# A linear-attention plus maxout-FFN kernel on one core: PSUM banks dealt by earliest predicted release, E and F loaded over the ACT queue, parts of the attention work moved

## The chip, the core and the metric

The kernel runs on one NeuronCore of a Trainium2 chip. The metric is device time in microseconds (us). The names are those of the profile: PE is TensorE's matrix multiply, PEld its weight load, DVE is VectorE, ACT is ScalarE, POOL is GpSimd, and SP is the engine that only issues DMAs here. The *granted clock* is the share of TensorE's full clock that the profile's records show. A run is "fast" unless its time is over 1.5% above the fastest run of the same kernel; only fast runs are compared.

## The reference

```python
# q, k, v: (8 batches, 8 heads, 1024, 64); E, F: (64, 1024)
k_proj = einsum('ks,bhsd->bhkd', E, k);  v_proj = einsum('ks,bhsd->bhkd', F, v)
attn   = softmax(q @ k_proj.T / sqrt(64))          # 64 keys only
x      = (attn @ v_proj), heads side by side       # (8192 tokens, 512)
h      = max(x @ w1, x @ w2, x @ w3)               # (8192, 768)
out    = h @ w_out                                 # (8192, 512)
```

The FFN is nearly all of the work: per batch 144 matmuls of 128x512 for w1 to w3 and 48 for w_out.

## The kernel before

Every engine's instruction order is written out by hand. A batch has two chunks of 512 tokens. A chunk has six *up* steps (12 matmuls each, into three PSUM banks) and four *down* steps (6 matmuls each, into one bank). Attention of the *next* batch is slipped in behind these steps by a plan: `(chunk, step): [work]`. The work items are `kproj`/`vproj` (multiply by E and F), `kt` and `qp` (transposes on PE), `qd` (four DVE copies into `q_p`, then a DMA transpose into `qT`), `sc` (scores, then exp on ACT), and `za` (sums and values on PE, reciprocal on ACT as ln and exp, multiply on DVE).

PE writes into eight PSUM banks. (The Trainium skill, "PSUM — Partial Sum Buffer", section "Specifications (TRN2)", gives 8 banks of 512 FP32 values per partition, and the kernel's tile has that shape.) A bank can be written again only when ACT or DVE has read it. The kernel deals the banks while it is built, with a small model of when each engine will be done (shortened here; `...` and the comments are mine):

```python
psum_t = psum.tile([P, 8, 512], FP32, name="banks")
clock = {"pe": 0.0, "s": 0.0, "v": 0.0}     # predicted time of PE, ACT, DVE
free = [0.0] * 8                            # predicted release of each bank

def two():                                  # an even-odd pair, for sums, values, scores, transposes
    n = min(range(0, 8, 2), key=lambda n: max(free[n:n + 2]))
    deal((n, n + 1)); return psum_t[:, n:n + 2, :], (n, n + 1)

def bank():                                 # one bank, for up, down, kproj, vproj
    def rank(n):
        ready = free[n] <= clock["pe"]
        return (not ready, ready and free[n ^ 1] <= clock["pe"], free[n])
    n = min(range(8), key=rank)
    deal((n,)); return psum_t[:, n, :], (n,)
...
def up(b, ch, jt):
    ...                                     # banks h[0], h[1], h[2], 4 matmuls each
    nc.scalar.copy(out=h1s, in_=h[0][0])    # ACT releases h[0]
    run_later()                             # ACT: exp of the scores dealt before
    nc.vector.tensor_tensor(out=m12, in0=h[1][0], in1=h1s, op=ALU.max)   # DVE releases h[1]
    most(hTs[b, ch][:, jt, :], *h[2], m12)                               # DVE releases h[2]
```

`rank` prefers a bank that is ready by the model and whose neighbour is *not* ready, so that whole pairs stay free for `two()`.

The program starts with the loads of E, F, q, k and v, dummy matmuls (`idle(n)`, each 128x512, into a bank that nobody reads) that are meant to keep PE's clock up, and attention for the first half chunk.

The softmax here doesn't subtract the row's maximum and nothing guards it: scores larger than these inputs give would overflow.

Of the kernel before, what the change touches and what calls it, by code (L numbers as in the profile page):

```python
# [15 lines left out]
def kernel(  # L16
# [13 lines left out]
    nc = tc.nc  # L30

    B, H, S, D = q.shape
    KP = E.shape[0]
# [4 lines left out]
    P = 128  # L38
# [25 lines left out]
    clock = {"pe": 0.0, "s": 0.0, "v": 0.0}  # L64
    free = [0.0] * 8
# [11 lines left out]
        return psum_t[:, n:n + 2, :], (n, n + 1)  # L77

    def bank():
        def rank(n):  # L80
            ready = free[n] <= clock["pe"]
            return (not ready, ready and free[n ^ 1] <= clock["pe"], free[n])

        n = min(range(8), key=rank)
        deal((n,))
        return psum_t[:, n, :], (n,)

# [14 lines left out]
    def copy(eng, o, i, ns=(), dt=0.65):  # L102
        {  # L103
            "v": nc.vector.tensor_copy, "s": nc.scalar.copy, "g": nc.gpsimd.tensor_copy
        }[eng](out=o, in_=i)
        runs(eng, clock["pe"] if ns else 0.0, dt, ns)
# [40 lines left out]
    q_c = [first.tile([P, 2, SPC, 2, D], BF16, name=f"q_c{i}") for i in range(2)]  # L147
    v_heads = [(0, 4), (4, 6), (6, 8)]
    v_f = [first.tile([P, b - a, SI, D], FP32, name=f"v_f{a}") for a, b in v_heads]
    for i in range(2):  # L150
        cols = slice(i * S // 2, (i + 1) * S // 2)
        nc.sync.dma_start(out=ef_f[0:KP, cols], in_=E[:, cols])
        nc.scalar.dma_start(out=ef_f[KP:P, cols], in_=F[:, cols])
    for i in range(2):
        nc.sync.dma_start(out=q_f[i], in_=view(q, 0)[:, 4 * i:4 * i + 4, 0:SPC])
    for i in range(2):
# [43 lines left out]
    def exps(b, g, lo, nsi, sc):  # L200
        t, ns, ready = sc
        pTs[b, g, lo] = att.tile([P, 2, CHUNK], BF16, name="pT", bufs=4)[:, :, 0:nsi * HALF]
        nc.scalar.activation(out=pTs[b, g, lo], in_=t, func=AF.Exp, scale=scale)  # L203
        runs("s", ready, 0.17 + nsi * 0.107, ns)
# [14 lines left out]
    def sums(b, g, lo, nsi):  # L219
        return pair_mm(b, g, lo, nsi, lambda rows, hp: ones[rows])  # L220

    def invert(b, g, lo, nsi, z):
        t, ns, ready = z
        zl = att.tile([P, 2, CHUNK], FP32, name="zl", bufs=1)[:, :, 0:nsi * HALF]
        nc.scalar.activation(out=zl, in_=t, func=AF.Ln)  # L225
        runs("s", ready, 0.17 + nsi * 0.107, ns)
        if nsi == SI:
            zi = att.tile([P, 2, CHUNK], FP32, name="zi", bufs=2)
        else:
            zi = att.tile([P, 2, CHUNK // 2], FP32, name="zi0", bufs=4)  # L230
        nc.scalar.activation(out=zi, in_=zl, func=AF.Exp, scale=-1.0)  # L231
        zis[b, g, lo] = zi, runs("s", ready, 0.17 + nsi * 0.107)

    def values(b, g, lo, nsi):
        if b not in xTs:
            xTs[b] = att.tile([P, NCT, SI, P], BF16, name="xT")
        return pair_mm(b, g, lo, nsi, lambda rows, hp: vps[b][rows, 2 * g + hp, :])

    def scale_x(b, g, lo, nsi, av):
        t, ns, ready = av  # L240
        zi, when = zis.pop((b, g, lo))
        nc.vector.tensor_tensor(  # L242
            out=xTs[b][:, g, lo:lo + nsi, :].rearrange("a (c s) p -> a c (s p)", c=2),
            in0=t, in1=zi, op=ALU.mult,
        )
        runs("v", max(ready, when), 0.17 + nsi * 0.13, ns)
# [8 lines left out]
    def sc(b, g, lo=0, nsi=SI):  # L255
        def f():
            t = scores(b, g, lo, nsi)
            later.append(lambda: exps(b, g, lo, nsi, t))
        return f
# [66 lines left out]
    def kproj(b):  # L326
        def f():
            t, ns = bank()
            proj(b, 1, t, (LO, HI), 4 * D)
            kps[b] = att.tile([P, 2, 2 * D], BF16, name="kp")  # L330
            copy("v", kps[b].rearrange("a g x -> a (g x)"), t[:, 0:4 * D], ns, 0.43)
        return f
# [31 lines left out]
    def idle(n):  # L364

        t, ns = bank()
        for _ in range(n):
            nc.tensor.matmul(out=t, lhsT=warm[:, 0:P], rhs=warm, start=True, stop=True)  # L368
        free[ns[0]] = pe(n * MM)
# [56 lines left out]
    def v_part(i):  # L426
        a, b = v_heads[i]
        t, ns = bank()
        proj(0, 2, t, (slice(a, b), slice(a, b)), (b - a) * D)
        copy("v", vps[0][:, a:b].rearrange("a h d -> a (h d)"), t[:, 0:(b - a) * D], ns, 0.4)  # L430

    C0 = (0, SPC)
    idle(8)
    cast_q(0, "v")
    cast_q(1, "s")
    turn_ef()
    turn_q(0)
    turn_q(1)
    idle(2)
    cast_q(2, "v")  # L440
    cast_q(3, "s")
    turn_q(2)
    turn_q(3)
    idle(8)
    cast_k(0, 0, "v")
    cast_k(0, 1, "s")
    kp = k_half(0)
# [3 lines left out]
    sc01 = [scores(0, g, *C0) for g in (0, 1)]  # L451
    for g in (0, 1):
        exps(0, g, *C0, sc01[g])
    idle(4)
    cast_k(1, 0, "v")
    cast_k(1, 1, "g")
    load_w(0, 0)
    load_w(0, 1)
    for g in (0, 1):
        invert(0, g, *C0, sums(0, g, *C0))  # L460
        idle(1)
    kp = k_half(1)
    idle(2)
    k_turn(1, kp)
    idle(2)
    sc23 = [scores(0, g, *C0) for g in (2, 3)]
    for g in (2, 3):
        exps(0, g, *C0, sc23[g - 2])
    copy("v", v_t[:, 0:2], v_f[0][:, 0:2])
    copy("g", v_t[:, 2:4], v_f[0][:, 2:4])  # L470
    load_w(1, 0)
# [2 lines left out]
    nc.gpsimd.dma_start(out=q_t[:, :, SPC:], in_=view(q, 0)[:, :, SPC:])  # L474
    load_w(2, 1)
    nc.gpsimd.dma_start(out=wout_sb, in_=moe_w_out.rearrange("(jt p) m -> p jt m", p=P))
    copy("v", v_t[:, 4:6], v_f[1])
    idle(1)
    v_part(0)
    idle(1)  # L480
    for g in (2, 3):
        invert(0, g, *C0, sums(0, g, *C0))
    idle(1)
    scale_x(0, 0, *C0, values(0, 0, *C0))
    copy("v", v_t[:, 6:8], v_f[2])
    v_part(1)
    scale_x(0, 1, *C0, values(0, 1, *C0))
# [104 lines left out]
    def ld(b):  # L592
        return lambda: load(b)

    def plan(b):
        n = b + 1
        if b == 0:
            c1 = (SPC, SPC)
            return {
                (0, 5): [za(0, 0, *c1), sc(0, 2, *c1)],  # L600
                (0, 6): [za(0, 1, *c1), sc(0, 3, *c1)],
                (0, 7): [za(0, 2, *c1)],
                (0, 8): [za(0, 3, *c1), ld(1)],
                (1, 0): [kproj(1)],
                (1, 1): [kt(1), qp(1, (0,)), qp(1, (1,))],
                (1, 2): [qp(1, (2,)), qp(1, (3,)), sc(1, 0), vproj(1), ld(2)],
                (1, 3): [za(1, 0), sc(1, 1)],
                (1, 4): [za(1, 1), sc(1, 2)],
                (1, 5): [za(1, 2), sc(1, 3)],
                (1, 7): [za(1, 3)],  # L610
            }
        if b == 1:
            return {
                (0, 1): [qd(2)],
                (0, 5): [kproj(2), vproj(2), ld(3)],
                (0, 6): [kt(2)],
                (0, 7): [sc(2, 0)],
                (0, 9): [za(2, 0), sc(2, 1)],
                (1, 1): [za(2, 1), sc(2, 2)],
                (1, 3): [za(2, 2), sc(2, 3)],  # L620
                (1, 5): [za(2, 3)],
            }
        if b == 2:
            return {
                (0, 0): [qd(3)],
                (0, 2): [kproj(3), vproj(3), ld(4)],
                (0, 3): [kt(3)],
                (0, 4): [sc(3, 0)],
                (0, 6): [za(3, 0), sc(3, 1)],
                (1, 0): [za(3, 1), sc(3, 2), qd(4)],  # L630
                (1, 2): [za(3, 2), sc(3, 3), kproj(4), vproj(4), ld(5)],
                (1, 4): [kt(4)],
                (1, 5): [za(3, 3), sc(4, 0)],
            }
        if n == B:
            return {}
        out = {
            (0, 1): [za(n, 0), sc(n, 1)],
            (0, 3): [za(n, 1), sc(n, 2)],
            (0, 9): [za(n, 2), sc(n, 3)],  # L640
            (1, 3): [za(n, 3)],
        }
        if n + 1 < B:
            out[0, 2] = [qd(n + 1)]
            out[0, 9] += [kproj(n + 1), vproj(n + 1)]
            out[1, 1] = [kt(n + 1)]
            out[1, 3] += [sc(n + 1, 0)]
        if n + 2 < B:
            out[1, 1] += [ld(n + 2)]
        return out  # L650

    for b in range(B):
        p = plan(b)

        def behind(ch, step):
            for f in p.get((ch, step), []):
                f()

        for ch in range(NCHUNK):
            if (b, ch) == (0, 0):  # L660
                c1 = (SPC, SPC)
                scale_x(0, 3, *C0, values(0, 3, *C0))
                up_first({
                    (2, 1): [qp(0, (0, 1), *c1), qp(0, (2, 3), *c1)],
                    (2, 2): [sc(0, 0, *c1)],
                    (2, 3): [sc(0, 1, *c1)],
                })
                run_later()
                behind(0, NJT - 1)
            else:  # L670
                for step in range(NJT):
                    up(b, ch, step)
                    behind(ch, step)
            for tt in range(SPC):
                down(b, ch, tt, "v" if (b, ch) == (0, 0) else "s")
                behind(ch, NJT + tt)
# [30 lines left out]
```

## Time and profile before

| | |
|---|---|
| time | 418.76 us, median of 3 runs (418.64 to 419.24); 418.51 to 420.86 in later rounds |
| span of the profiled run | 416.7 us |
| PE busy | 397.6 us, 95% |
| first FFN matmul | 23.53 us |

The head of the profile's page, and its line of the chain of work that ended last (shares of the span by engine):

```profile
span 416.7 us, 6032 instructions
## 1 busy us (share of the span) xinstructions
PE 397.6 (95%) x2400; PEld 180.8 (43%) x2445; DVE 203.9 (49%) x315; ACT 193.5 (46%) x280; POOL 27.9 (7%) x37
...
PE 87%; ACT 5%; DVE 3%; DMA 2%; issue 2%; SPq 1%; DVEq 0%; ACTq 0%
```

PE is the bottleneck, so the question is what PE waits for. The waits view of PE (who waited for whom: us in total, times, longest):

```profile
PE banks L499 <- ACT zl L225: 2.1, 3, 0.7
PE banks L212 <- ACT pT L203: 1.7, 4, 0.5
PE banks L499 <- DVE vp L103: 1.5, 2, 0.8
PE banks L375 <- DMA ef_f<-in_F_dram: 1.2, 1, 1.2
...
PE banks L499 <- issue: 0.8, 5, 0.2
PE banks L284 <- DVE qT L103: 0.8, 1, 0.8
...
PE banks L192 <- ACT pT L203: 0.5, 1, 0.5
```

Here L499 is `up`, L212 sums and values, L192 scores, L375 the transposes of E and F, L284 the q transposes. A wait of `up` for "ACT zl" is a wait for a *bank*: zl is made by reading the sums' bank.

The timeline before (start, length, engine, line, operation, out<-in; in brackets the idle time before it and what ended it). The start of the program:

```profile
6.00 1.13 PE L375 MATMUL banks<-ident_f,ef_f 128*128 128x128 f32 x8 [1.20 <-DMA ef_f<-in_F_dram]
...
11.06 0.69 DVE L103 CAST k_t<-k_f_92 128x1024 bf16<-128x1024 f32 x1 [0.88 <-DMA k_f_92<-in_k_dram]
...
23.53 13.17 PE L499 MATMUL banks<-xT,w_sb 128*128 128x512 bf16 x59
```

Then the last batch, b = 7, where there is no attention at all:

```profile
375.90 0.69 DVE L509 TENSOR_TENSOR hT<-banks,m_3390 128x512 bf16<-128x512 f32 x1
376.65 2.47 PEld L499 LDWEIGHTS <-w_sb 128*128 128x128 bf16 x12 [0.20 <-issue]
...
378.57 0.69 DVE L509 TENSOR_TENSOR hT<-banks,m_3407 128x512 bf16<-128x512 f32 x1
379.32 2.47 PEld L499 LDWEIGHTS <-w_sb 128*128 128x128 bf16 x12 [0.20 <-issue]
```

The weight loads start anew at 376.65 and 379.32. That is 0.06 us after the DVE instruction that releases the previous step's last bank has ended (375.90 + 0.69 = 376.59, and 378.57 + 0.69 = 379.26). A step takes 379.32 - 376.65 = 2.67 us, and its twelve matmuls alone need 12 x 0.216 = 2.59 (24 back-to-back ones take 5.18 us in the chain of waits). The idle label says only "issue", and no waits line is longer than 0.2 us.

### The profile page before, as it was taken

What the parts mean: (1) busy time and instruction counts of PE and PEld (TensorE: products, weight loads), DVE (VectorE), ACT (ScalarE), POOL (GpSimd) and SP (SyncE); (2) the same over time, 40 slices, a digit from 0 to 9 for tenths busy, and PEclk for the clock granted to TensorE, in tenths of its full rate; (3) what the DMA queues carried; (4) which work ended last, traced back from release to release, by engine and by line L of the source; (5) the groups of instructions that cost most, each with busy time, mean ns of one, the idle gap of its engine ahead of it and who ended that gap; (6) DMA issues with size and microseconds to landing.
All of it is one profiled execution on the core that took longest, in us unless ns stands there. A gap on an engine that the chain in (4) does not pass through costs nothing.

```text
span 416.7 us, 6032 instructions
## 1 busy us (share of the span) xinstructions
PE 397.6 (95%) x2400; PEld 180.8 (43%) x2445; DVE 203.9 (49%) x315; ACT 193.5 (46%) x280; POOL 27.9 (7%) x37
## 2 busy tenths in 40 slices
PE   6999998999999999999999999999999999999996
PEld 3444453344444444444544435443454444444442
DVE  3357664464373636637263464527365272525251
ACT  2530617822764266457535546436445456432322
POOL 0621001002000200200200001000000000000000
PEclk9999999999999999999999999999999999999999
DMA  7999949958922699599793159921410202020202
GB/s 259 353 205 196 178 124 164 202 135 122 242 46 101 126 197 248 95 227 219 116 241 86 66 109 224 172 103 31 122 50 2 101 0 102 0 102 0 101 2 101
DMA packets 58492, 54.92 MB, mean 132 GB/s; under 512 B 25952, under 2 KB 51808, under 8 KB 58464
## 3 DMA queue, kind: packets, MB, share of 16 engines
q0 software_dynamic: 25296, 25.69, 39.3%
q1 hardware_dynamic: 33008, 28.58, 20.6%
q8 instruction: 19, 0.31, 0.3%
q10 hardware_dynamic: 160, 0.26, 0.2%
q14 instruction: 9, 0.07, 0.1%
HBM read 57.15 MB, written 16.78 MB: 177 GB/s over the span
## 4 chain that ended last, share of the span: by engine, by line
PE 87%; ACT 5%; DVE 3%; DMA 2%; issue 2%; SPq 1%; DVEq 0%; ACTq 0%
PE banks L499 58%; PE banks L574 19%; PE banks L212 4%; PE banks L273 4%; ACT zl L225 2%; DMA k_f_92<-in_k_dram 2%; PE banks L192 1%; ACT pT L203 1%; PE banks L368 1%; PE banks L284 1%; ACT zi L231 1%; DVE vp L103 1%; ACT o_sb L103 0%; ACT h1s L557 0%; DVE q_p L103 0%
## 5 line engine op out<-in xcount | busy, mean ns | idle before, releaser
L499 PE MATMUL banks<-xT,w_sb 128*128 128x512 bf16 x1119 | 255.1, 379 | 6.1 <-ACT zl L225 2.1
L499 PEld LDWEIGHTS <-w_sb 128*128 128x128 bf16 x1152 | 110.0, 98 | 143.2 <-issue 15.5
L557 ACT COPY h1s<-banks 128x512 f32<-128x512 f32 x90 | 52.5, 584 | 95.1 <-PE banks L499 90.7
L574 PE MATMUL banks<-wout_sb,hT 128*128 128x512 bf16 x375 | 86.1, 379 | 1.0 <-DVE vp L103 0.2
L242 DVE TENSOR_TENSOR xT<-banks,zi 128x1024 bf16<-128x1024 f32 x28 | 34.3, 1225 | 74.4 <-ACT zi L231 52.5
L103 ACT COPY o_sb<-banks 128x512 f32<-128x512 f32 x60 | 35.1, 585 | 54.8 <-PE banks L574 54.8
L574 PEld LDWEIGHTS <-hT 128*128 128x128 bf16 x384 | 36.5, 98 | 47.2 <-issue 4.6
L225 ACT ACTIVATE zl<-banks 128x1024 f32<-128x1024 f32 (+1 forms) x36 | 33.5, 930 | 31.3 <-PE banks L212 30.3
L203 ACT ACTIVATE pT<-banks 128x1024 bf16<-128x1024 f32 (+1 forms) x36 | 33.3, 931 | 14.6 <-PE banks L192 14.6
L231 ACT ACTIVATE zi<-zl 128x1024 f32<-128x1024 f32 x28 | 29.6, 1057 | 0.9
L178 POOL DMA_DIRECT2D q_t<-in_q_dram x7 | 6.2, 879 | 199.3 <-DMA qT<-q_p 64.1
L273 PEld LDWEIGHTS <-efT 128*64 128x64 bf16 x304 | 14.6, 110 | 5.2 <-issue 4.7
L212 PE MATMUL banks<-pT,ones 64*64 64x512 bf16 (+1 forms) x144 | 13.7, 374 | 1.9 <-ACT pT L203 1.7
L192 PE MATMUL banks<-qT,kpT 64*64 64x512 bf16 (+1 forms) x144 | 13.0, 359 | 0.7 <-ACT pT L203 0.5
L212 PE MATMUL banks<-pT,vp 64*64 64x512 bf16 (+1 forms) x144 | 13.3, 356 | 0.2 <-DVE vp L103 0.2
L368 PE MATMUL banks<-warm 128*128 128x512 bf16 x34 | 11.1, 440 | 1.5 <-DVE warm L162 1.2
L212 PEld LDWEIGHTS <-ones 64*64 64x64 bf16 x144 | 4.4, 103 | 15.5 <-issue 13.8
L273 PE MATMUL banks<-v_t,efT 128*64 128x256 bf16 (+1 forms) x160 | 9.6, 263 | 0.4 <-DVE v_t L103 0.3
L103 ACT CAST vp<-banks 64x256 bf16<-64x256 f32 x14 | 5.1, 365 | 10.4 <-PE banks L273 10.2
L273 PE MATMUL banks<-k_t,efT 128*64 128x256 bf16 (+1 forms) x144 | 8.9, 264 | 0.6 <-DVE k_t L103 0.5
L103 DVE CAST vp<-banks 64x256 bf16<-64x256 f32 (+2 forms) x17 | 7.0, 410 | 4.4 <-ACT vp L103 3.7
L103 DVE COPY q_p<-q_t 128x1024 bf16<-128x1024 bf16 x24 | 8.5, 419 | 0.0
(252 smaller groups left out, 219.1 us busy)
## 6 DMA issues: line engine op xcount, KB each, us to landing
out_dram<-o_sb SPq DMA_DIRECT2D x30, 512.0 KB, 3.3
k_t<-in_k_dram POOLq DMA_DIRECT2D x7, 1024.0 KB, 14.0
q_t<-in_q_dram POOLq DMA_DIRECT2D x7, 1024.0 KB, 9.8
v_t<-in_v_dram POOLq DMA_DIRECT2D x7, 1024.0 KB, 17.8
w_sb<-in_moe_w_dram POOLq DMA_DIRECT2D x6, 384.0 KB, 7.9
k_f_92<-in_k_dram SPq DMA_DIRECT2D x1, 1024.0 KB, 7.9
k_f_93<-in_k_dram SPq DMA_DIRECT2D x1, 1024.0 KB, 10.0
v_f_96<-in_v_dram SPq DMA_DIRECT2D x1, 1024.0 KB, 11.5
```

The costliest lines, as they stand in the source:

```text
L103: {"v": nc.vector.tensor_copy, "s": nc.scalar.copy, "g": nc.gpsimd.tensor_copy}[eng](out=o, in_=i)
L192: nc.tensor.matmul(out=t[c * HALF:(c + 1) * HALF, hp, 0:n * P], lhsT=kpTs[b][rows, g, :], rhs=qTs[b][rows, at:at + n, :], start=True, stop ...
L203: nc.scalar.activation(out=pTs[b, g, lo], in_=t, func=AF.Exp, scale=scale)
L212: nc.tensor.matmul(out=t[hp * HALF:(hp + 1) * HALF, c, 0:nsi * HALF], lhsT=w(rows, hp), rhs=p[rows, hp, :], start=True, stop=True,)
L225: nc.scalar.activation(out=zl, in_=t, func=AF.Ln)
L231: nc.scalar.activation(out=zi, in_=zl, func=AF.Exp, scale=-1.0)
L242: nc.vector.tensor_tensor(out=xTs[b][:, g, lo:lo + nsi, :].rearrange("a (c s) p -> a c (s p)", c=2), in0=t, in1=zi, op=ALU.mult,)
L273: nc.tensor.matmul(out=t[hh * HALF:(hh + 1) * HALF, 0:width], lhsT=efT[:, si, kv - 1, :], rhs=qkv[b][kv][:, heads[hh], si, :], start=(si = ...
L368: nc.tensor.matmul(out=t, lhsT=warm[:, 0:P], rhs=warm, start=True, stop=True)
L499: nc.tensor.matmul(out=h, lhsT=w_sb[i][:, ct, jt * P:(jt + 1) * P], rhs=xTs[b][:, ct, ch * SPC:(ch + 1) * SPC, :], start=(ct == 0), stop=( ...
L557: nc.scalar.copy(out=h1s, in_=h[0][0])
L574: nc.tensor.matmul(out=o_ps, lhsT=hTs[b, ch][:, jt, tt * P:(tt + 1) * P], rhs=wout_sb[:, jt, :], start=(jt == 0), stop=(jt == NJT - 1),)
```

## The change

Its intent: take the bank that has been free longest; take the two E issues off SP, so that q and k are issued sooner; and start attention of b = 1 one step earlier, with scores two steps ahead of their sums. It also moves `qd` (the q copies on DVE) in b = 3 to 5 from step 2 to step 4. In the prologue, `k_half(1)` goes ahead of the sums, and the dummies are shared out anew. The diff, whole:

```diff
--- before.py
+++ after.py
@@ -77,11 +77,7 @@
         return psum_t[:, n:n + 2, :], (n, n + 1)
 
     def bank():
-        def rank(n):
-            ready = free[n] <= clock["pe"]
-            return (not ready, ready and free[n ^ 1] <= clock["pe"], free[n])
-
-        n = min(range(8), key=rank)
+        n = min(range(8), key=lambda n: free[n])
         deal((n,))
         return psum_t[:, n, :], (n,)
 
@@ -147,10 +143,8 @@
     q_c = [first.tile([P, 2, SPC, 2, D], BF16, name=f"q_c{i}") for i in range(2)]
     v_heads = [(0, 4), (4, 6), (6, 8)]
     v_f = [first.tile([P, b - a, SI, D], FP32, name=f"v_f{a}") for a, b in v_heads]
-    for i in range(2):
-        cols = slice(i * S // 2, (i + 1) * S // 2)
-        nc.sync.dma_start(out=ef_f[0:KP, cols], in_=E[:, cols])
-        nc.scalar.dma_start(out=ef_f[KP:P, cols], in_=F[:, cols])
+    nc.scalar.dma_start(out=ef_f[0:KP], in_=E)
+    nc.scalar.dma_start(out=ef_f[KP:P], in_=F)
     for i in range(2):
         nc.sync.dma_start(out=q_f[i], in_=view(q, 0)[:, 4 * i:4 * i + 4, 0:SPC])
     for i in range(2):
@@ -430,18 +424,18 @@
         copy("v", vps[0][:, a:b].rearrange("a h d -> a (h d)"), t[:, 0:(b - a) * D], ns, 0.4)
 
     C0 = (0, SPC)
-    idle(8)
+    idle(9)
     cast_q(0, "v")
     cast_q(1, "s")
     turn_ef()
     turn_q(0)
     turn_q(1)
-    idle(2)
+    idle(3)
     cast_q(2, "v")
     cast_q(3, "s")
     turn_q(2)
     turn_q(3)
-    idle(8)
+    idle(7)
     cast_k(0, 0, "v")
     cast_k(0, 1, "s")
     kp = k_half(0)
@@ -451,21 +445,20 @@
     sc01 = [scores(0, g, *C0) for g in (0, 1)]
     for g in (0, 1):
         exps(0, g, *C0, sc01[g])
-    idle(4)
+    idle(2)
     cast_k(1, 0, "v")
     cast_k(1, 1, "g")
     load_w(0, 0)
     load_w(0, 1)
-    for g in (0, 1):
-        invert(0, g, *C0, sums(0, g, *C0))
-        idle(1)
     kp = k_half(1)
-    idle(2)
+    z01 = [sums(0, g, *C0) for g in (0, 1)]
+    invert(0, 0, *C0, z01[0])
     k_turn(1, kp)
     idle(2)
     sc23 = [scores(0, g, *C0) for g in (2, 3)]
-    for g in (2, 3):
-        exps(0, g, *C0, sc23[g - 2])
+    exps(0, 2, *C0, sc23[0])
+    invert(0, 1, *C0, z01[1])
+    exps(0, 3, *C0, sc23[1])
     copy("v", v_t[:, 0:2], v_f[0][:, 0:2])
     copy("g", v_t[:, 2:4], v_f[0][:, 2:4])
     load_w(1, 0)
@@ -474,14 +467,13 @@
     nc.gpsimd.dma_start(out=q_t[:, :, SPC:], in_=view(q, 0)[:, :, SPC:])
     load_w(2, 1)
     nc.gpsimd.dma_start(out=wout_sb, in_=moe_w_out.rearrange("(jt p) m -> p jt m", p=P))
+    idle(3)
+    v_part(0)
     copy("v", v_t[:, 4:6], v_f[1])
-    idle(1)
-    v_part(0)
-    idle(1)
     for g in (2, 3):
         invert(0, g, *C0, sums(0, g, *C0))
-    idle(1)
     scale_x(0, 0, *C0, values(0, 0, *C0))
+    idle(2)
     copy("v", v_t[:, 6:8], v_f[2])
     v_part(1)
     scale_x(0, 1, *C0, values(0, 1, *C0))
@@ -601,12 +593,13 @@
                 (0, 6): [za(0, 1, *c1), sc(0, 3, *c1)],
                 (0, 7): [za(0, 2, *c1)],
                 (0, 8): [za(0, 3, *c1), ld(1)],
-                (1, 0): [kproj(1)],
-                (1, 1): [kt(1), qp(1, (0,)), qp(1, (1,))],
-                (1, 2): [qp(1, (2,)), qp(1, (3,)), sc(1, 0), vproj(1), ld(2)],
-                (1, 3): [za(1, 0), sc(1, 1)],
-                (1, 4): [za(1, 1), sc(1, 2)],
-                (1, 5): [za(1, 2), sc(1, 3)],
+                (0, 9): [kproj(1)],
+                (1, 0): [kt(1), qp(1, (0,)), qp(1, (1,))],
+                (1, 1): [sc(1, 0), qp(1, (2,)), qp(1, (3,))],
+                (1, 2): [vproj(1), sc(1, 1), sc(1, 2), ld(2)],
+                (1, 3): [za(1, 0), sc(1, 3)],
+                (1, 4): [za(1, 1)],
+                (1, 5): [za(1, 2)],
                 (1, 7): [za(1, 3)],
             }
         if b == 1:
@@ -641,7 +634,7 @@
             (1, 3): [za(n, 3)],
         }
         if n + 1 < B:
-            out[0, 2] = [qd(n + 1)]
+            out[0, 4] = [qd(n + 1)]
             out[0, 9] += [kproj(n + 1), vproj(n + 1)]
             out[1, 1] = [kt(n + 1)]
             out[1, 3] += [sc(n + 1, 0)]
@@ -661,8 +654,8 @@
                 c1 = (SPC, SPC)
                 scale_x(0, 3, *C0, values(0, 3, *C0))
                 up_first({
-                    (2, 1): [qp(0, (0, 1), *c1), qp(0, (2, 3), *c1)],
-                    (2, 2): [sc(0, 0, *c1)],
+                    (2, 1): [qp(0, (0, 1), *c1)],
+                    (2, 2): [qp(0, (2, 3), *c1), sc(0, 0, *c1)],
                     (2, 3): [sc(0, 1, *c1)],
                 })
                 run_later()
```

## The prediction

> **What bounds the kernel.** TensorE. The page's busy table has PE busy 397.6 of 416.7 us, the chain of waits gives it 87% of the span, and the granted clock is 1.00. Only time in which PE does nothing useful can be won. The timeline shows it in four places.
> 1. Prologue: the first FFN matmul starts at 23.5 us, after four SP issues (two of E, two of q, 0.6 us each), the first k tile (issued at 3.16, landed at 11.06) and attention for the first half chunk.
> 2. First chunk (23.5 to 50): PE waits 0.8 us for a DVE qT copy before the second pair of q transposes, 0.5 us for pT.
> 3. Attention of b=1 (50 to 81.4): the waits view lists three waits of 0.47 us for pT (sums one step after the scores) and 0.77 us for vp, whose bank was dealt before its four casts (1.6 us in all) were over. 31.4 us go where the matmuls, at 0.216 us per 128x512, need about 27.5.
> 4. Later: three waits of 0.69 us for ACT zl, at (0,3) of b=3, 4, 5, where 1.42 us of q_p copies sit on DVE ahead of the bank releases (b=6, without a qd, has none); one more vp wait of 0.77 (141 us); a dozen of 0.2 us.
>
> **What the change does.** Hardly any work is added or removed; it moves waits.
> - E and F on ACT take 1.2 us of issue off SP, so k is issued that much sooner. But from 5 us on the DMA engines are full (share 1.0, 320 to 410 GB/s in the windows view), and the Trainium skill ("DMA: Bandwidth & Descriptors", "Issuing engines are not separate DMA queues") says that issuing elsewhere saves only sequencer time; 2.5 MB still precede k. k should land 0.4 to 0.8 us sooner, and with k_half(1) ahead of the sums the FFN start 0.6 to 1.0 us sooner (about 22.7). The weights landed 2 us or more ahead of use.
> - Splitting the q transposes over (2,1) and (2,2) removes the 0.8 us wait: net 0.8.
> - b=1 one step earlier, scores two steps ahead of sums: the pT waits (1.4) and the vp wait (0.8) go, but ACT, busy 8.8 of 10 us at 70 to 80, gets two exps at once and some bank waits return: net 1.3.
> - qd at (0,4): the three zl waits, net 1.9 of 2.1.
> - Banks by earliest predicted release: takes the longest-free bank, so mispredicted releases (vp) cost less: 0.8 at 141 us, 0.4 elsewhere; but pairs are broken up, so some scores or sums will wait for two banks: minus 1.
>
> Sum 0.8 + 0.8 + 1.3 + 1.9 + 1.2 - 1.0 = 5.0, hardly any hidden, as PE is the chain; I take 4.6 for what I cannot see. Predicted 414.2 us, range 411.0 to 417.2. Faster by over 2%: 0.08; within 2%: 0.90; slower by over 2%: 0.02.
>
> **What would show it.** First FFN matmul at 22.5 to 23; k_t cast at 10.3 to 10.7; no zl waits at (0,3); no vp wait of 0.77; the pT waits gone from 50 to 80, some replaced by waits for zl or xT; PE busy nearly unchanged while the span shrinks.
>
> **What would make it wrong.** E/F landing late behind q; the v tile of b=1 (landed 57.1) now asked for at about 58, so a late one stalls vproj; fragmented pairs adding a bank wait in every batch (0.5 us x 6), which would cancel half; an idle stretch lowering the clock.

## The result and the profile after

The changed kernel takes **415.07 us** (median of 4 runs, 414.92 to 415.52); the kernel before in the same rounds 419.0 (418.64 to 420.86). The ratio is **0.9899**, 95% interval 0.9869 to 0.993: a ratio here is the mean time of one kernel's fast runs over that of the other's fast runs of the same rounds, so not quite the ratio of the medians quoted. The prediction was 414.2 (411.0 to 417.2).

So the total was right. The profile after says that hardly any term of my sum was. Its head, and its chain by engine:

```profile
span 413.7 us, 6017 instructions
## 1 busy us (share of the span) xinstructions
PE 396.6 (96%) x2397; PEld 181.4 (44%) x2442; DVE 204.4 (49%) x315; ACT 192.4 (47%) x280; POOL 27.7 (7%) x37
...
PE 87%; ACT 4%; DVE 3%; issue 3%; DMA 2%; ACTq 0%; DVEq 0%
```

PE's waits after (`up` is now L491, `down` L566, the E and F transposes L369, sums and values L206, scores L186):

```profile
PE banks L369 <- DMA ef_f<-in_F_dram: 3.8, 1, 3.8
PE banks L566 <- DVE hT L501: 2.8, 4, 0.9
PE banks L362 <- DVE warm L156: 1.2, 1, 1.2
PE banks L491 <- issue: 0.6, 4, 0.2
PE banks L206 <- ACT pT L197: 0.6, 2, 0.3
PE banks L186 <- ACT pT L197: 0.5, 1, 0.5
```

The waits for zl and the two long ones for vp are gone. Those for pT are halved, from 2.2 to 1.1 us: the three of b = 1 went. Two are new or larger: 3.8 us for E and F, and three of 0.86 us for hT. The start of the program after, in the timeline:

```profile
9.05 1.94 PE L369 MATMUL banks<-ident_f,ef_f 128*128 128x128 f32 x8 [3.83 <-DMA ef_f<-in_F_dram]
...
12.03 1.05 ACT L99 CAST k_t<-k_f_92 128x1024 bf16<-128x1024 f32 x1
...
14.32 0.99 DVE L99 CAST k_t<-k_f_92 128x1024 bf16<-128x1024 f32 x1
...
25.75 13.12 PE L491 MATMUL banks<-xT,w_sb 128*128 128x512 bf16 x59
```

The FFN starts 25.75 - 23.53 = 2.2 us *later*. The last batch after:

```profile
370.77 13.11 PE L491 MATMUL banks<-xT,w_sb 128*128 128x512 bf16 x58
370.99 12.40 PEld L491 LDWEIGHTS <-w_sb 128*128 128x128 bf16 x58
```

There is no break from step to step any more; the ACT copies that begin each step come 2.59 us apart (374.42 and 377.01 in the timeline) where there were 2.67.

Since PE's order is fixed, the time divides well by marks on PE: the first FFN matmul, and the first `up` after each chunk's `down`. In us, from the timelines of all fast profiles ("b0" to "b7" are batches):

| kernel | start of FFN | b0 | b1+b2 | b3 to b5 | b6+b7 | span |
|---|---|---|---|---|---|---|
| before | 23.53 | 57.89 | 99.65 | 144.48 | 91.15 | 416.7 |
| changed | 25.75 | 55.69 | 97.89 | 144.11 | 90.26 | 413.7 |
| difference | +2.22 | -2.20 | -1.76 | -0.37 | -0.89 | -3.0 |

These columns are a better instrument than the times. Where two kernels share the code of a column, the columns of different runs agreed within 0.15 us (except one b1+b2 of 98.52, with a 0.4 us wait for a v tile), while the start varies by over half a microsecond from run to run (25.75 and 25.19 for two profiles of the changed kernel). The kernel before has only this one profile, of one of its quicker runs (418.44 us; its timed runs lie at 418.5 to 420.9), so gains read from the columns come out smaller than those from the times. The experiments' columns:

| run | start of FFN | b0 | b1+b2 | b3 to b5 | b6+b7 | span |
|---|---|---|---|---|---|---|
| e0 changed, again | 25.19 | 55.70 | 97.89 | 144.12 | 90.30 | 413.2 |
| e1 E, F as before | 24.66 | 55.70 | 97.89 | 144.13 | 90.22 | 412.6 |
| e2 E, F in halves on ACT | 25.65 | 55.70 | 97.89 | 144.13 | 90.23 | 413.6 |
| e3 E, F whole on SP | 25.02 | 55.70 | 97.89 | 144.13 | 90.36 | 413.1 |
| e4 27 dummies | 24.42 | 55.70 | 97.91 | 144.12 | 90.25 | 412.4 |
| e5 before + bank rule | 23.89 | 56.87 | 97.90 | 144.49 | 90.25 | 413.4 |
| e6 qd back at step 2 | 25.29 | 55.70 | 97.98 | 144.50 | 90.33 | 413.8 |
| e7 qd at step 6 | 25.32 | 55.73 | 98.52 | 140.99 | 90.34 | 410.9 |
| e8 plan back | 25.69 | 56.86 | 97.88 | 144.12 | 90.35 | 414.9 |
| e10 27 dummies, qd at 6 | 23.66 | 55.71 | 97.88 | 141.00 | 90.35 | 408.6 |
| e11 before + rule + qd at 6 | 23.40 | 56.86 | 97.89 | 140.99 | 90.26 | 409.4 |

### The profile page after: what moved, and what is told of

It is laid out like the page before. It is cut to its first block, busy times and chain, and to the rows that moved or that the text cites. A ratio compares the mean times of both kernels' runs of the same rounds, so it can differ in the third digit from the quotient of the medians.

```text
span 413.7 us, 6017 instructions
## 1 busy us (share of the span) xinstructions
PE 396.6 (96%) x2397; PEld 181.4 (44%) x2442; DVE 204.4 (49%) x315; ACT 192.4 (47%) x280; POOL 27.7 (7%) x37
## 3 DMA queue, kind: packets, MB, share of 16 engines
q0 software_dynamic: 25296, 25.69, 39.1%
## 4 chain that ended last, share of the span: by engine, by line
PE 87%; ACT 4%; DVE 3%; issue 3%; DMA 2%; ACTq 0%; DVEq 0%
PE banks L491 56%; PE banks L566 19%; PE banks L206 4%; PE banks L267 4%; PE banks L186 2%; DMA ef_f<-in_F_dram 2%; PE banks L362 1%; ACT zl L219 1%; ACT zi L225 1%; DVE q_p L99 1%; ACT pT L197 1%; PE banks L278 1%; DVE hT L501 1%; PE banks L369 0%; PE banks L390 0%
## 5 line engine op out<-in xcount | busy, mean ns | idle before, releaser
L491 PE MATMUL banks<-xT,w_sb 128*128 128x512 bf16 x1119 | 253.6, 379 | 2.0 <-issue 0.6
L491 PEld LDWEIGHTS <-w_sb 128*128 128x128 bf16 x1152 | 109.9, 98 | 137.1 <-issue 9.7
L566 PE MATMUL banks<-wout_sb,hT 128*128 128x512 bf16 x375 | 86.6, 379 | 3.5 <-DVE hT L501 2.8
L566 PEld LDWEIGHTS <-hT 128*128 128x128 bf16 x384 | 36.4, 98 | 49.6 <-DVE hT L501 6.3
L206 PE MATMUL banks<-pT,ones 64*64 64x512 bf16 (+1 forms) x144 | 13.8, 375 | 1.1 <-ACT pT L197 0.6
L186 PE MATMUL banks<-qT,kpT 64*64 64x512 bf16 (+1 forms) x144 | 13.5, 359 | 0.9 <-ACT pT L197 0.5
L206 PE MATMUL banks<-pT,vp 64*64 64x512 bf16 (+1 forms) x144 | 13.4, 355 | 0.2 <-DVE vp L99 0.2
L206 PEld LDWEIGHTS <-ones 64*64 64x64 bf16 x144 | 4.2, 103 | 14.2 <-issue 14.0
```

What stands on the lines that cost most here:

```text
L186: nc.tensor.matmul(out=t[c * HALF:(c + 1) * HALF, hp, 0:n * P], lhsT=kpTs[b][rows, g, :], rhs=qTs[b][rows, at:at + n, :], start=True, stop ...
L206: nc.tensor.matmul(out=t[hp * HALF:(hp + 1) * HALF, c, 0:nsi * HALF], lhsT=w(rows, hp), rhs=p[rows, hp, :], start=True, stop=True,)
L491: nc.tensor.matmul(out=h, lhsT=w_sb[i][:, ct, jt * P:(jt + 1) * P], rhs=xTs[b][:, ct, ch * SPC:(ch + 1) * SPC, :], start=(ct == 0), stop=( ...
L566: nc.tensor.matmul(out=o_ps, lhsT=hTs[b, ch][:, jt, tt * P:(tt + 1) * P], rhs=wout_sb[:, jt, :], start=(jt == 0), stop=(jt == NJT - 1),)
```

## The experiments

Twelve kernels ran, all with correct results. Times are medians of the fast runs; "before" is the kernel before in the same rounds.

### The bank rule alone (e5), with the changed kernel beside it (e0)

```diff
 # on the kernel before; nothing else
-        def rank(n): ...
-        n = min(range(8), key=rank)
+        n = min(range(8), key=lambda n: free[n])
```

> The kernel before with only the bank rule changed. Theory: the rule is the larger part of the gain after 81 us: it takes away the vp waits of 0.77 us and the 0.08 us by which each step of up was longer (the two chunks of b = 7 take 15.7 and 15.5 us instead of 16.0 and 15.8), 2 to 3 us in all, ratio 0.993 to 0.995. Rival: the gain came from the plan and from qd; then the ratio is 0.998 or more and the last batch takes as long as before. Whether the zl waits of 0.69 us in b = 3, 4, 5 go with the rule alone is open: if they do, moving qd was not needed.

> The changed kernel itself, as the reference of its variants within these rounds: ratio to the kernel before 0.988 to 0.992, as on record. Its three waits of 0.86 us for hT (the first down step of chunk 0 in b = 3, 4, 5) and the E and F transposes at about 9 us should be seen again.

Measured: e5 415.23 us, ratio 0.9898 (0.9869 to 0.9926); e0 415.3 us, ratio 0.9899 (0.9876 to 0.9921); before 419.52. **One line gives the whole net gain of the change.** It was worth more than even this theory said (0.993 to 0.995). The columns show where: 57.89 to 56.87 in b0, 99.65 to 97.90 in b1+b2, 91.15 to 90.25 in b6+b7, 3.7 us in all; and nothing in b3 to b5. In those three batches the zl waits did not go with the rule. They moved from `up` (0.69 us) to the scores (L188 in this run), as PE's waits of e5 show:

```profile
PE banks L188 <- ACT zl L221: 2.9, 3, 1.0
```

Scores need a pair of banks, so this is the cost of broken pairs that I had predicted, and it is hidden in the column. In b = 4, counted from the batch's first `up`, ACT's h1s copies start at the same time in both kernels until 9.71 us. The next one comes at 13.93 us before and at 14.34 in e5. By the batch's last `o_sb` copy the 0.4 us are made up (47.07 in both). So these three batches lose about 3 x 0.4 us to pairs, beyond the old wait (an estimate from the one timeline), and win as much back in their other steps.

In the last batch of e5 the weight loads run without the break at each step, and the ACT copies come 2.59 us apart (376.72 and 379.31), as in the changed kernel:

```profile
373.93 9.16 PEld L495 LDWEIGHTS <-w_sb 128*128 128x128 bf16 x43
```

Why is the rule worth so much in b = 7, where nobody asks for a pair? The dealing can be printed while the kernel is built. It is the kernel's own prediction, not a measurement. Of the 379 single banks dealt in the whole program, by how long before (in the model) the bank had been released:

```
rule                         not yet   under 0.2 us   0.2 to 1 us   over 1 us
ready, neighbour busy first     9          39             124          207
earliest release first          5           1              39          334
```

A typical deal in the first chunk of b = 7, old rule: bank 0, predicted to be released 0.11 us ago, while banks 2 to 7 had been free for 1.0 to 11.2 us. Its neighbour had just been dealt, so it came first. The old rule took its own prediction for exact, and gave PE a bank at the very moment of release. On the chip that moment is the end of the DVE instruction plus the 0.06 us until the weight load starts again (the lines of the last batch above). That costs 0.08 us at four of the six steps of a chunk here, 0.3 us per chunk. And where the prediction is wrong by more, it costs more. After `vproj` the model lets two ACT and two DVE copies run side by side; in the timeline they ran one after the other, 0.74 + 0.87 us. The two vp waits of 0.77 us came from that; e5 has neither, though its copies still run one after the other.

### Where qd stands (e6, e7)

```diff
 # on the changed kernel
-            out[0, 4] = [qd(n + 1)]
+            out[0, 2] = [qd(n + 1)]     # e6
+            out[0, 6] = [qd(n + 1)]     # e7
```

> The changed kernel with qd back at step 2 of chunk 0. If moving qd removed the zl waits (my prediction), they return, 3 x 0.69 us, while the three hT waits of 0.86 us go: the time stays within 0.6 us of the changed kernel. If the bank rule had removed them already, nothing returns and the kernel gains up to 2.6 us, so that moving qd was a loss.

> The changed kernel with qd after the first down step of chunk 0 (step 6), where DVE has no bank to release for some 5 us. Theory: the wait only moved from zl to hT because the 1.42 us of q_p copies stand before the last hT. Then both waits are gone: 2.0 to 2.6 us less than the changed kernel, with the DMA transpose still landed long before the scores that read it. Rival: DVE is full there as well and the copies delay something else (the o_sb or xT chain), then less than 1 us is won.

Measured: e6 415.73 us, ratio 0.991 (0.9888 to 0.9933), against 0.9899 for the changed kernel beside it; b3 to b5 144.50 instead of 144.12. So the move that I had priced at 1.9 us is worth 0.4. e7 412.13 us, ratio 0.9821 (0.9793 to 0.9849); b3 to b5 140.99, which is 3.1 us less than 144.12. This beat its expectation of 2.0 to 2.6.

The cause is in the timeline. First the kernel before, around step 3 of chunk 0 in b = 4:

```profile
239.64 1.42 DVE L103 COPY q_p<-q_t 128x1024 bf16<-128x1024 bf16 x4
...
240.98 0.68 DVE L561 TENSOR_TENSOR m_2310<-banks,h1s 128x512 f32<-128x512 f32 x1
...
242.09 1.24 PE L499 MATMUL banks<-xT,w_sb 128*128 128x512 bf16 x5 [0.69 <-ACT zl L225]
```

The changed kernel, around the first `down` of the same chunk:

```profile
243.90 1.42 DVE L99 COPY q_p<-q_t 128x1024 bf16<-128x1024 bf16 x4
...
246.02 0.69 DVE L501 TENSOR_TENSOR hT<-banks,m_2358 128x512 bf16<-128x512 f32 x1
...
246.77 4.28 PE L566 MATMUL banks<-wout_sb,hT 128*128 128x512 bf16 x18 [0.86 <-DVE hT L501]
```

And e7, the same place:

```profile
243.86 5.34 PE L566 MATMUL banks<-wout_sb,hT 128*128 128x512 bf16 x24
244.07 0.69 DVE L501 TENSOR_TENSOR hT<-banks,m 128x512 bf16<-128x512 f32 x1
244.68 1.42 DVE L99 COPY q_p<-q_t 128x1024 bf16<-128x1024 bf16 x4
```

DVE takes its work here in the order in which it was written: in the changed kernel h1s of the last step was ready at 243.73 us, but DVE took up m_2358, which reads it, only at 245.24, as the copies were ending. At step 2 the copies delayed the release of banks before a step that wants six of them. At step 4 they stand ahead of the last two results of the chunk, and the first `down` needs the last hT. In the `down` steps DVE has nothing to release, and there 1.42 us cost nothing.

### E and F: sharing, packet size, or PE's clock (e1 to e4)

```diff
 # each on the changed kernel
 # e1: as before: column halves, E on nc.sync, F on nc.scalar
 # e2: column halves, all four on nc.scalar
 # e3: whole rows, both on nc.sync ahead of q
-    nc.scalar.dma_start(out=ef_f[0:KP], in_=E)
-    nc.scalar.dma_start(out=ef_f[KP:P], in_=F)
+    nc.sync.dma_start(out=ef_f[0:KP], in_=E)
+    nc.sync.dma_start(out=ef_f[KP:P], in_=F)
 # e4: loads as in the change, but
-    idle(9)
+    idle(27)
```

> The changed kernel with only the E and F loads put back (halves, E on SP, F on ACT). Theory: the loads of E and F alone made the prologue 2.2 us longer (the transposes of E and F started at 9.05 us instead of 6.00, and then ran at half speed). Then the transposes start near 6.0 us, the first FFN matmul at 22.5 to 23.2 us instead of 25.7, and the kernel takes 412.0 to 412.8 us, 2.2 to 3 us less than the changed kernel. Rival: the reordered prologue is itself slower; then the first FFN matmul stays at 24.5 us or later although E and F land at 6.

> The changed kernel with E and F in halves as before (2 KB rows), but all four on ACT. If the rows of 4 KB are what made E and F slow, the transposes start before 7.5 us. If it is that E and F now share the DMA engines with q, which has a queue of its own and starts at the same time, they still start at 8.5 us or later.

> The changed kernel with E and F whole (4 KB rows) but on SP, ahead of q. If sharing with q is the cause, E and F land first: transposes at 5.5 to 6.5 us, first FFN matmul at 22.5 to 23.5. If the 4 KB rows are slow by themselves, transposes start at 7.5 us or later.

> The changed kernel with 27 dummy matmuls at the start instead of 9, so that PE is busy until E and F land at 9.0 us. Theory: part of the loss is that PE, idle for 3.8 us, comes back at half speed (eight transposes of E and F 417 ns each instead of 276). Then with the dummies those take about 276 ns again, and the first FFN matmul comes 0.8 to 1.8 us sooner (about 24.5). If the slowness has another cause they stay at 417 ns and nothing is won.

| run | time, us | ratio (95%) | E/F transposes start | first FFN matmul |
|---|---|---|---|---|
| changed (earlier rounds) | 415.07 | 0.9899 (0.9869 to 0.993) | 9.05 | 25.75 |
| e1 | 414.1 | 0.9859 (0.9834 to 0.9884) | 6.65 | 24.66 |
| e2 | 416.18 | 0.9914 (0.9886 to 0.9941) | 9.60 | 25.65 |
| e3 | 414.25 | 0.9853 (0.982 to 0.9886) | 5.38 | 25.02 |
| e4 | 414.06 | 0.9862 (0.9836 to 0.9888) | 9.29 | 24.42 |

Before was 420.14 in these rounds. The intervals of e1, e3 and e4 overlap that of the changed kernel a little; the gain of about 0.4%, 1.5 us, rests on three kernels agreeing on it. In the same rounds e2, as late as the change, took 415.4 to 417.18 us, and no run of e1, e3 or e4 took over 414.86.

*What made E and F late.* Not the size of the rows: in halves of 2 KB on ACT (e2) they are as late, and whole on SP (e3) they are there first. It is the sharing with q. Ahead of q on the SP queue, E went first. On the ACT queue, E and F move side by side with q's 1 MB from the SP queue. The Trainium skill describes both halves of this ("DMA: Bandwidth & Descriptors"): the issuing engines' queues run on the same 16 DMA engines and interleave (section "Issuing engines are not separate DMA queues"), and each DMA engine goes round-robin between the queues (section "Queues, rings and completion order"). The trace agrees: in the changed kernel E and F landed 5.2 and 7.6 us after issue, and q's two halves 5.4 and 7.7. In the kernel before, F alone on ACT and in halves took 4.0 us (median), and E on SP 3.5. No run has both on ACT with q held back, so a slower ACT queue is not wholly ruled out as a part of it. I had taken from the skill only that a move saves issue time. I overlooked that a place in a queue is also a priority: off the queue, E lost its precedence over q.

*What the lateness cost.* In e4 E and F are as late as in the change (9.29 us), and yet the FFN starts at 24.42. The prologues of the other runs support it: the five profiles with the change's own (changed, e0, e6, e7, e8) start the FFN at 25.19 to 25.75, the two with 27 dummies (e4, e10) at 24.42 and 23.66, the three with the old one (before, e5, e11) at 23.40 to 23.89. By the means of these groups the dummies win back 1.4 of the 1.8 us. So the larger part of the loss is not the lateness itself. It is that PE, idle for 3.8 us, comes back at a lower clock. The transposes of E and F, by tile (duration in ns: min/median/max, first and last start), first in the kernel before:

```profile
L375 PE MATMUL banks<-ident_f,ef_f x8: 274/276/348, 6.0 to 6.9; 128*128 128x128 f32 x8
```

In the changed kernel:

```profile
L369 PE MATMUL banks<-ident_f,ef_f x8: 417/417/449, 9.0 to 10.6; 128*128 128x128 f32 x8
```

In e4, with the dummies up to 8.9 us:

```profile
L369 PE MATMUL banks<-ident_f,ef_f x8: 274/276/347, 9.3 to 10.1; 128*128 128x128 f32 x8
```

That it is the clock is seen in e2, where they took the same 417 ns and the granted clock is on record. Its windows view from 9 to 12 us (busy us by engine, then the granted clock, here 0.55):

```profile
9.00:12.00 3.00, 2.40 (x15) 2.36 (x16) 0.69 (x1) 0.41 (x1) 0.00 (x0) 0.55 1.05 405
```

After the slow transposes come the q transposes, also slow (1.06 us for eight instead of 0.62), and DVE, in order behind them, casts the first k tile only at 14.32 although it had landed by 12.03. The skill ("TensorE: Matmul & The Clock Gate", section "What's actually happening") says that PE's clock is halved after an idle window of about 3.4 us and is full again after about as long a busy one. The runs agree in kind: e4, with no wait of PE over 0.35 us just before, kept its clock. In detail the idle stretch may be a little shorter: e6 had the slow 417 ns transposes after a wait of 3.16 us.

*Where e1 and e3 missed.* I expected the FFN at 22.5 to 23.5 with E and F early; it was 24.66 and 25.02, and e1 took 414.1 us instead of 412.0 to 412.8. By its start e1 met the mark of its rival, a slower prologue. Two things. First, e1 lost its clock too, after gaps of only 1.45 and 1.02 us. The windows view of e1, 9 to 12 us (granted clock 0.52), and under it that of e3:

```profile
9.00:12.00 3.00, 3.00 (x20) 2.05 (x19) 1.94 (x5) 1.05 (x2) 0.00 (x0) 0.52 1.03 379
9.00:12.00 3.00, 2.67 (x18) 1.15 (x16) 1.65 (x5) 0.62 (x1) 0.00 (x0) 1.00 1.00 367
```

e3 kept it (1.00, and eight q transposes in 0.62 us), though its gap before the first q transposes was longer, 1.74 us, and PE was no busier from 6 to 9 us (1.26 us against 1.32 in e1). So what decides after gaps of this length is open. Second, and this bounds both, the second k tile: its cast on POOL began at 15.00 and 15.36 us there, and at 13.79 in the kernel before. From that cast to the FFN it is 9.66 us in both e1 and e3, and 23.53 - 13.79 = 9.74 before. So the reordered prologue is not slower, and it wins about nothing; the chain hangs on that tile, whatever stands between. Why it landed 1.2 us later in e1 is open: e1 and e5 issue the same first loads in the same order, and in e5 the cast began at 14.08. The runs of the kernel before in those rounds differ by up to 1.8 us among themselves as well (418.67 to 420.48), so one profile of the prologue is not to be trusted to a microsecond.

### The plan of b = 0 (e8)

```diff
 # on the changed kernel: the plan of b = 0 and the q transposes at (2, 1) as before
-                (0, 9): [kproj(1)],
-                (1, 0): [kt(1), qp(1, (0,)), qp(1, (1,))],
-                ...
+                (1, 0): [kproj(1)],
+                (1, 1): [kt(1), qp(1, (0,)), qp(1, (1,))],
+                ...
```

> The changed kernel with the plan of b = 0 and the two q transposes of the first chunk put back. With the bank rule alone (on the kernel before) the first two chunks took 26.40 + 30.47 = 56.87 us, and in the changed kernel 55.69, so the plan should be worth about 1.2 us: chunks 0 and 1 at 56.6 to 57.1 us, the pT waits of 0.47 us back, the kernel 1.0 to 1.5 us slower than the changed one (ratio to before 0.992 to 0.994). My prediction had 2.1 us for it. If the pT waits were covered anyway, the time stays the same.

Measured: 415.85 us, ratio 0.9911 (0.989 to 0.9933). b0 takes 56.86 us, just as with the bank rule alone (56.87), and 55.70 with the plan. So the plan is worth 1.2 us, and the two effects add. The times show less of it than the 1.0 to 1.5 us expected: e8 is 0.6 us behind e0 and 0.8 behind the changed kernel's first runs, all in different rounds, and its ratio is 0.9911 where 0.992 to 0.994 was expected. The waits that the plan removes are back in PE's waits of e8:

```profile
PE banks L206 <- ACT pT L197: 2.0, 5, 0.5
...
PE banks L278 <- DVE qT L99: 0.8, 1, 0.8
```

### Together (e9, e10, e11)

```diff
 # e9:  changed kernel + E and F as before + idle(14) + qd at step 6
 # e10: changed kernel + idle(27) + qd at step 6
 # e11: kernel before + bank rule + qd at step 6, nothing else
```

> The changed kernel with the three repairs: E and F loaded as before, 14 dummies so that PE is not idle until they land, qd at step 6. Separate gains of 1.3 to 2 us (loads and clock) and 3.1 us (qd): first FFN matmul at 23 to 24 us, each of b = 3, 4, 5 at 47.0 us, time 410.5 to 411.5, ratio to before 0.978 to 0.981. If the gains overlap it stays at 0.982, as with qd at 6 alone.

> The changed kernel with E and F left on ACT, 27 dummies and qd at step 6. First FFN matmul at about 24.4 us as with the dummies alone; 0.5 to 1 us slower than with the loads put back, ratio 0.980 to 0.982. If it is as fast, keeping PE's clock up is all that the late loads cost.

> The kernel before with two lines changed only: the bank rule and qd at step 6. If bank rule and qd are the whole matter, it gains the rule's 4.3 us and the three scores waits of 0.97 us: 411.5 to 412.5 us, ratio 0.981 to 0.984, better than the whole change and about 1.2 us behind the version with the plan as well. Rival: the rule and the qd step need the other parts of the change, then it stays near 0.988.

| run | time, us | ratio (95%) |
|---|---|---|
| e9 | 409.96 | 0.9776 (0.9752 to 0.98) |
| e10 | 410.68 | 0.9797 (0.9769 to 0.9825) |
| e11 | 412.1 | 0.9821 (0.9799 to 0.9843) |

Before was 419.31. e11 came in as expected. e9 and e10 came out slightly better than their ranges (410.5 to 411.5 us for e9, ratio 0.980 to 0.982 for e10); e10's FFN started at 23.66 instead of about 24.4. e9 beats both kernels: 2.2% faster than the kernel before, and about 5 us faster than the changed kernel (medians of different rounds). Four of its five runs took 409.74 to 410.72; its first, the profiled one (424.26 us, granted clock 0.95), is left out of every comparison, so e9 has no timeline here. e11 shows that two lines on the kernel before give more than the whole change. e10 against e9 leaves about 0.7 us (medians) for E and F being late with the clock kept up, but their intervals overlap.

## Why the prediction was right, and where its terms were wrong

The predicted 414.2 us is 0.9 from the measured 415.07, but that was luck: the sum was right because errors cancelled.

| term | predicted gain | measured | by |
|---|---|---|---|
| prologue: E, F on ACT, reordering | 0.8 | -1.3 to -2.2 | starts 25.19, 25.75 against 23.53, 23.89 |
| q transposes split; b = 1 plan | 0.8 + 1.3 | 1.2 | e8, and e5 against changed |
| qd at (0,4) | 1.9 | 0.4 | e6 |
| bank rule | 0.8 + 0.4 - 1.0 = 0.2 | 3.7 in the columns; 4.3 in the times | e5 |

- **Bank rule: the term that failed most.** The mechanism that I gave it, mispredicted releases, is real: the two vp waits are 1.5 of the 3.7 us, and one of them I had credited to the plan. "Pairs are broken up, so some scores or sums will wait for two banks: minus 1" was about right too: scores wait 0.97 us for a pair in b = 3 to 5, where an `up` step had waited 0.69. But the columns there did not grow (144.48 and 144.49). What failed is that I counted only waits that the waits view lists, while the old rule's steady cost, up to 0.08 us per `up` step, falls below its lines. With a few waits of 0.2 us it makes up the rest of the gain, about 2.2 us (by subtraction), and it pays for the pairs besides.
- **Prologue: wrong in sign.** The prediction named its own failure under what would make it wrong: "E/F landing late behind q" and "an idle stretch lowering the clock". Both came, and I had given them no weight in the sum.
- **qd: the mechanism was right, the consequence was not.** "The three zl waits, net 1.9 of 2.1": the zl waits did go, but the same 1.42 us of copies then held up hT, 3 x 0.86 us. I asked what the copies would stop delaying and not what they would delay.
- **Plan: mechanism right, size too large.** The pT waits of b = 1 and the qT wait went, as said. The 0.8 us of vp in that term belonged to the bank rule, which removes them without the plan.
- Right without reserve: PE is the bottleneck and its busy time nearly unchanged (397.6 and 396.6 us); weights and the v tile of b = 1 were in time.

## What to carry to other kernels

When buffers are dealt by a predicted release, take the one free longest: a prediction that is right to 0.1 us still costs the time from the reader's end to the next writer's start (0.06 us here) each time if the buffer is taken at its moment of release, and this loss hides below what a list of waits shows. Measure it instead by the period of a regular stretch against the sum of its matmuls. When work on an in-order engine is moved, look at what then stands behind it, and put it where the engine has nothing to release. And moving a load to another queue changes its place in line as well as who issues it.

## What the Trainium skill lacked or had wrong

- "DMA: Bandwidth & Descriptors", section "Issuing engines are not separate DMA queues", is right that the queues interleave, but says that issuing on several engines only saves issue time. Neither it nor the section on queues draws the consequence that a move also changes precedence: the transposes of E and F started at 5.38 us with E and F ahead of q on SP, and at 9.05 with them on ACT.
- "TensorE: Matmul & The Clock Gate", section "HAM oscillation — how this bites in real kernels", gives the rule of no PE gaps over about 3.4 us. The clock was also lost after a wait of 3.16 us (e6, transposes of 417 ns), and in e1 after gaps of 1.45 and 1.02 us close to each other: granted clock 0.52 from 9 to 12 us. In e3 it was kept after one of 1.74 us. (The page's next section allows for frequent short gaps; it gives no length that would tell e1 from e3.)
- The granted clock of a profile can miss it: the changed kernel's profile gives 1.00 for 9 to 12 us, where its transposes took 417 ns instead of 276. The same page warns that these records are unreliable; the durations settle it.
- No page that I read has the cost of reusing a PSUM bank right at its release: weight loads resume 0.06 us after the releasing DVE instruction ends, and a step of 2.59 us becomes 2.67.
